# Retention: the decays move from the output to the query, the state's copy, k and the mask

## The chip, the cores and the metric

The kernel runs on one core of one Trainium2 chip. The metric is the device time of one execution in microseconds, the median of three runs.

## The reference

The inputs are q, k and v of shape (8, 8, 576, 64): batch, heads, sequence, head size. Retention is attention with a decay in place of the softmax. It is followed by two feed-forward layers without biases.

```python
scores = scale * np.matmul(q, k.transpose(0, 1, 3, 2))
gamma = 1.0 - 2.0 ** (-5.0 - np.arange(H, dtype=np.float32))
Dmat = np.where(rel >= 0, gamma[:, None, None] ** rel[None, :, :], 0.0)   # rel = i - j
att = np.matmul(scores * Dmat[None], v)          # then to (4608, 512)
h = x @ w_in
x = (h * np.cos(h)) @ w_out                      # 512 -> 2048 -> 512
h = np.maximum(np.maximum(x @ w1, x @ w2), x @ w3)
out = h @ w_out2                                 # 512 -> 768 -> 512
```

## The kernel before

The 4608 tokens are cut into nine blocks of 512. In each block the eight heads are taken as four pairs, so retention consists of 36 units (block j, pair hp), numbered 4j + hp. Inside a unit the tokens are cut into chunks of 128; where a sequence of 576 ends inside a block, two of the chunks are of 64. Blocks 0, 2, 4, 6 and 8 have four chunks, blocks 1, 3, 5 and 7 have three full ones and two short ones.

Because gamma^(i-j) is a product, the kernel never forms the whole decay matrix. Per unit it does this:

- `att_load` (L486) brings q and k by feature and k and v by token into one tile `u`.
- `att_scale` (L492, GpSimd) multiplies v by gamma to the minus position.
- `att_scores` (L504, TensorE) forms the scores of each chunk in PSUM, and `att_mask` (L513, VectorE) multiplies them by a mask of ones and zeros into `ret`.
- `att_state` (L547, TensorE) adds each chunk's product of k and v to a running state in PSUM, and `att_keep` (L531, ScalarE) copies the state out before each chunk for its queries.
- `att_out` (L563 and L575, TensorE) forms the output `po` from `ret` and v and from the kept states and q.
- `att_decay` (L590, VectorE) reads `po` out of PSUM, one instruction for each chunk, and multiplies by gamma to the position of the row; that is the scaled output `k_x`.

The feed-forward products run in one level of Strassen's scheme (seven products of quarters), and each operand is split into a high and a low part. `build_in` takes the differences of quarters (L356, GpSimd in most blocks), rounds them to the high part (L360, ScalarE) and subtracts to get the low part (L364, VectorE). `group_in` runs the products (L385), whose results ScalarE copies (L418, L423, L430, L400) or VectorE adds up (L410). `gate` forms h * cos(h): L448 and L457 on ScalarE, L452 and L460 on VectorE, L453 on GpSimd. Weights are read raw, joined (L176 and L177, VectorE), summed (L183, GpSimd), combined (L190 to L193, VectorE) and split (L200 to L207 on ScalarE, L212 and L216).

The order of the work on each engine is written out by hand. `at(n, fn)` puts a step n slots ahead, and `tick()` issues all steps that are due; each product of `group_in` is one slot. The first 15 slots have no product: units 0 to 4 and the first weights fill them. A unit with start s has its scaling in slot s - 1 (but not before the present one), its scores in s, its mask in s + 1, its states from s + 1 on, its output in s + 5 and its decays in s + 6. Two units start every seven slots. Each engine works through its own list in order.

Of the kernel before, what the change touches and what calls it, by code (L numbers as in the profile page):

```python
# [14 lines left out]
AF = mybir.ActivationFunctionType  # L15
ALU = mybir.AluOpType

B, H, S, D = 8, 8, 576, 64
T = B * S
DM = H * D  # L20
NB = 512
HB = NB // 2
NBLK = T // NB
NPAIR = H // 2
CH = 128
# [14 lines left out]
def chunks_of(j):  # L40

    t0 = j * NB
    cut = (-t0) % S
    segs = [(0, cut), (cut, NB)] if 0 < cut < NB else [(0, NB)]
    out = [(a, min(CH, e - a)) for s, e in segs for a in range(s, e, CH)]
    full = [c for c in out if c[1] == CH]
    short = [c for c in out if c[1] < CH]  # L50
    assert len(short) in (0, 2) and all(n == CH // 2 for _, n in short)
    order = full + short
    col = {a: sum(n for _, n in order[:i]) for i, (a, _) in enumerate(order)}
    return [(a, n, col[a], (t0 + a) % S) for a, n in out]


def column_tokens(j):

    idx = np.zeros(NB, np.int64)
    for a, n, c, _ in chunks_of(j):  # L60
        idx[c : c + n] = j * NB + a + np.arange(n)
    return idx


CG = 0
CM = CG + NPAIR * CH
CM2 = CM + CH
CGS = CM2 + CH
CTV = CGS + NPAIR * 9
NCONST = CTV + NBLK * NPAIR * 8  # L70


def constants():
    gamma = (1.0 - 2.0 ** (-5.0 - np.arange(H, dtype=np.float32))).astype(np.float64)
    c = np.zeros((128, NCONST), np.float64)
    p = np.arange(128)
    for hp in range(NPAIR):
        g = gamma[2 * hp + p // 64]
        c[:, CG + hp * CH : CG + (hp + 1) * CH] = g[:, None] ** np.arange(CH) / math.sqrt(D) / WSCALE
        c[:, CGS + hp * 9 : CGS + (hp + 1) * 9] = g[:, None] ** (64 * np.arange(9))  # L80
    c[:, CM : CM + CH] = np.arange(CH)[None, :] >= p[:, None]
    c[:, CM2 : CM2 + CH] = c[:, CM : CM + CH] * ((np.arange(CH) // 64)[None, :] == (p // 64)[:, None])
    for j in range(NBLK):
        pos = (column_tokens(j) % S).reshape(NB // CH, CH)
        for hp in range(NPAIR):
            for s in range(4):
                for e in range(2):
                    col = CTV + ((j * NPAIR + hp) * 4 + s) * 2 + e
                    c[:, col] = gamma[2 * hp + e] ** (-pos[s].astype(np.float64))
    return c.astype(np.float32)  # L90
# [11 lines left out]
def retention_ffn(ctx: ExitStack, tc: tile.TileContext, att, w_in, w_out, w123, w_out2, cst, out):  # L102
    nc = tc.nc
# [12 lines left out]
    def x4(name, shape, dt=F32):  # L116
        return xpool.tile([128, *shape], dt, tag="x", name=name)

    def bank(name):
        return ps.tile([128, NB], F32, tag="b", name=name)  # L120
# [16 lines left out]
    def at(n, fn):  # L137
        agenda.setdefault(slot[0] + n, []).append(fn)
# [329 lines left out]

    cs = cpool.tile([128, NCONST], F32, name="cs")
    units = {}  # L470
    quarters_of = {}

    def order_of(n):
        return divmod(n, NPAIR)
# [12 lines left out]

    def att_scale(n):

        v = units[n]["kv"][:, 1].rearrange("p (s d) -> p s d", d=64)  # L490
        col = CTV + n * 8
        nc.gpsimd.tensor_tensor(  # L492
            out=v, in0=v, in1=cs[:, col : col + 8].unsqueeze(2).to_broadcast([128, 8, 64]), op=ALU.mult
        )

    def att_scores(n):
        u = units[n]
        qT, kT = u["qk"][:, 0], u["qk"][:, 1]
        u["sc"] = [bank(f"sc{n}_{e}") for e in range(2)]
        for s in range(NB // CH):  # L500
            sl = slice(s * CH, (s + 1) * CH)
            for e in range(2):
                r = slice(64 * e, 64 * e + 64)
                nc.tensor.matmul(u["sc"][e][:, sl], kT[r, sl], qT[r, sl], start=True, stop=True)  # L504

    def att_mask(n):
        u = units[n]
        nfull = sum(m == CH for _, m, _, _ in chunks_of(order_of(n)[0]))
        for e in range(2):
            for at_, k, col in ((0, nfull, CM), (nfull, NB // CH - nfull, CM2)):  # L510
                if k:
                    sl = slice(at_ * CH, (at_ + k) * CH)
                    nc.vector.tensor_tensor(  # L513
                        out=u["ret"][:, e, sl].rearrange("p (s i) -> p s i", i=CH),
                        in0=u["sc"][e][:, sl].rearrange("p (s i) -> p s i", i=CH),
                        in1=cs[:, col : col + CH].unsqueeze(1).to_broadcast([128, k, CH]),
                        op=ALU.mult,
                    )

    def att_keep(n, i):  # L520

        u = units[n]
        j, hp = order_of(n)
        ch = chunks_of(j)
        if i >= len(ch):
            return
        _, m, _, pos = ch[i]
        st = state[:, hp * CH : (hp + 1) * CH]
        if pos:
            um = u["kept"][i] = u["um"][:, len(u["kept"])]  # L530
            nc.scalar.copy(um, st)  # L531
        if pos + m == S:
            nc.scalar.activation(st, cs[:, CM : CM + CH], AF.Copy, scale=0.0)

    def att_state(n, i):

        u = units[n]
        j, hp = order_of(n)
        ch = chunks_of(j)
        if i >= len(ch):  # L540
            return
        kn, v = u["kv"][:, 0], u["kv"][:, 1]
        _, m, c, pos = ch[i]
        if pos + m < S:
            s, p = divmod(c, CH)
            sl = slice(s * CH, (s + 1) * CH)
            nc.tensor.matmul(  # L547
                state[:, hp * CH : (hp + 1) * CH],
                kn[p : p + m, sl],
                v[p : p + m, sl],  # L550
                start=False,
                stop=True,
                skip_group_check=True,
            )

    def att_out(n):
        u = units[n]
        j, hp = order_of(n)
        qT, v = u["qk"][:, 0], u["kv"][:, 1]
        po = u["po"] = bank(f"po{n}")  # L560
        for s in range(NB // CH):
            for e in range(2):
                nc.tensor.matmul(  # L563
                    po[64 * e : 64 * e + 64, s * CH : (s + 1) * CH],
                    v[:, s * CH + 64 * e : s * CH + 64 * e + 64],
                    u["ret"][:, e, s * CH : (s + 1) * CH],
                    start=s == 0,
                    stop=False,
                    skip_group_check=True,
                )  # L570
        for i, um in u["kept"].items():
            _, m, c, _ = chunks_of(j)[i]
            for e in range(2):
                r = slice(64 * e, 64 * e + 64)
                nc.tensor.matmul(  # L575
                    po[r, c : c + m], um[r, r], qT[r, c : c + m], start=False, stop=True, skip_group_check=True
                )

    def att_decay(n):
        u = units.pop(n)  # L580
        j, hp = order_of(n)
        o = quarters_of.setdefault(j, {"name": f"x{j}", "n": NB})
        half = f"k{hp // 2 + 1}"
        if half not in o:
            o[half] = x4(f"{half}_x{j}", [2, NB])
        for _, m, c, pos in chunks_of(j):
            t, cc = divmod(c, HB)
            g = CGS + hp * 9 + pos // 64
            at_ = (hp % 2) * HB + cc
            nc.vector.scalar_tensor_tensor(  # L590
                out=o[half][:, t, at_ : at_ + m],
                in0=u["po"][:, c : c + m],
                scalar=cs[:, g : g + 1],
                in1=cs[:, CG + hp * CH : CG + hp * CH + m],
                op0=ALU.mult,
                op1=ALU.mult,
            )

    def att_unit(n, start):

        at(max(0, start - 1), lambda: att_scale(n))
        at(start, lambda: att_scores(n))
        at(start, lambda: att_keep(n, 0))
        at(start + 1, lambda: att_mask(n))
        for i in range(5):
            at(start + i + 1, lambda i=i: att_state(n, i))
            if i < 4:
                at(start + i + 1, lambda i=i: att_keep(n, i + 1))
        at(start + 5, lambda: att_out(n))
        at(start + 6, lambda: att_decay(n))  # L610

    NUNIT = NBLK * NPAIR

# [74 lines left out]
    for n in range(5):  # L688
        att_unit(n, 2 * n)
# [10 lines left out]
    for k in range(1, NUNIT - 4):  # L700
        if k > 1:
            at(max(0, start_of(k) - 4), lambda k=k: att_load(4 + k))
        att_unit(4 + k, start_of(k))
    for j in range(1, NBLK):
        k = 4 * (j - 1)
# [288 lines left out]
```

## Time and profile before

| what | value |
|---|---|
| median of 3 runs | 1521.58 us (1521.57 to 1521.79) |
| profiled execution, first to last instruction (span) | 1516.2 us |
| median of the runs less the span | 5.4 us |
| TensorE matmul busy | 1454.9 us, 96% |
| VectorE busy | 1224.6 us, 81% |
| ScalarE busy | 726.8 us, 48% |
| GpSimd busy | 268.7 us, 18% |
| mean granted TensorE clock | 0.988 |

The span is counted on the chip's own instructions in one profiled execution; the runs' times also hold what lies before and after them. Busy shares are means over a kernel with several stages: retention with the first half of the first layer comes first, then the rest of that layer, then the second.

### The profile page before, as it was taken

The page shows a single profiled execution, that of the slowest core. Times are in us where ns is not written, and L with a number is a line of the kernel's source. Part 1 is how long each engine was busy: PE and PEld are TensorE (multiplying, and loading weights), DVE is VectorE, ACT ScalarE, POOL GpSimd, SP SyncE. Part 2 cuts the span into 40 slices and gives each one's busy share as a digit, 9 for nine tenths or more (in the row PEclk, how much of TensorE's full clock was granted, in tenths as well). Part 3 has the DMA queues.
Part 4 walks back from the last instruction along what each step waited for, and adds up shares of the span by engine and source line. Part 5 has one row for each costly group of instructions (what it writes and reads, how often), then busy time and mean ns, then how long its engine had stood idle before and what let it go on. Part 6 is the DMA issues. An engine that isn't in the chain of part 4 may idle for free.

```text
span 1516.2 us, 30767 instructions
## 1 busy us (share of the span) xinstructions
PE 1454.9 (96%) x12506; PEld 1416.0 (93%) x12506; DVE 1224.6 (81%) x1759; ACT 726.8 (48%) x1214; POOL 268.7 (18%) x216
## 2 busy tenths in 40 slices
PE   6899999999899997899999999999999999999998
PEld 5798989998889997899999999999999999999998
DVE  6888999989889989999999998656664555538997
ACT  3555555556667755454445444334432333323332
POOL 3344444444222001100000000000000000004221
PEclk9899999999999998999999999999999999999999
DMA  7588888876989984556555568923431110254443
GB/s 292 181 292 304 309 300 301 318 290 240 355 304 364 328 294 156 184 193 215 193 203 195 196 216 323 397 107 119 147 127 48 70 66 34 70 191 163 168 168 138
DMA packets 83084, 324.46 MB, mean 214 GB/s; under 512 B 9216, under 2 KB 9216, under 8 KB 76928
## 3 DMA queue, kind: packets, MB, share of 16 engines
q1 hardware_dynamic: 82944, 322.51, 59.4%
q8 instruction: 98, 1.61, 0.4%
q14 instruction: 42, 0.34, 0.1%
HBM read 190.35 MB, written 132.12 MB: 213 GB/s over the span
## 4 chain that ended last, share of the span: by engine, by line
PE 46%; DVE 6%; issue 3%; DMA 2%; ACT 1%; POOL 0%; DVEq 0%; SPq 0%; ACTq 0%; POOLq 0%
PE wo L795 17%; PE d_b L385 14%; PE b_b L385 7%; PE o L795 4%; PE a_b L385 3%; DVE l_m L768 1%; DMA st_o<-p_o 1%; DVE tb_m L356 1%; DVE o_o L808 1%; DVE x_m L759 1%; DVE u_o L808 1%; DMA raw_b<-w 1%; DVE l_g L768 0%; DMA k_m<-mq 0%; ACT h_m L763 0%
## 5 line engine op out<-in xcount | busy, mean ns | idle before, releaser
L795 PE MATMUL wo<-h_g,w_wo 128*128 128x256 f32 x1728 | 314.9, 284 | 0.0
L795 PEld LDWEIGHTS wo<-h_g,w_wo 128*128 128x128 f32 x1728 | 271.3, 193 | 0.0
L795 PE MATMUL wo<-l_g,w_wo 128*128 128x256 f32 x864 | 246.6, 285 | 7.6 <-DVE l_g L768 7.6
L385 PE MATMUL d_b<-x_z,w_b 128*128 128x256 f32 x1944 | 248.8, 283 | 2.9 <-ACT s_b L430 2.1
L385 PEld LDWEIGHTS d_b<-x_z,w_b 128*128 128x128 f32 x1944 | 239.9, 192 | 3.7 <-ACT s_b L430 2.7
L795 PEld LDWEIGHTS wo<-l_g,w_wo 128*128 128x128 f32 x864 | 166.7, 193 | 9.6 <-DVE l_g L768 9.5
L385 PE MATMUL b_b<-x_z,w_b 128*128 128x256 f32 x972 | 131.6, 283 | 2.0 <-DVE x_z L364 2.0
L385 PE MATMUL d_a<-x_x,w_wi 128*128 128x256 f32 x864 | 123.2, 293 | 4.1 <-DVE x_x L364 2.9
L385 PEld LDWEIGHTS b_b<-x_z,w_b 128*128 128x128 f32 x972 | 123.2, 192 | 2.2 <-DVE x_z L364 2.2
L385 PE MATMUL d_a<-x_y,w_wi 128*128 128x256 f32 x864 | 115.3, 291 | 9.2 <-ACT s_a L418 5.8
L385 PEld LDWEIGHTS d_a<-x_y,w_wi 128*128 128x128 f32 x864 | 110.9, 199 | 10.4 <-ACT s_a L418 6.5
L385 PEld LDWEIGHTS d_a<-x_x,w_wi 128*128 128x128 f32 x864 | 110.2, 195 | 8.9 <-DVE x_x L364 4.1
L795 PE MATMUL o<-h_m,w_o 128*128 128x256 f32 x648 | 117.5, 283 | 0.0
L763 ACT CAST h_g<-tb_g 128x1024 fp32r<-128x1024 f32 x36 | 37.8, 1051 | 150.5 <-DVE tb_g L356 145.9
L795 PEld LDWEIGHTS o<-h_m,w_o 128*128 128x128 f32 x648 | 101.1, 192 | 0.0
L452 DVE SCALAR_TENSOR_TENSOR t_a<-s_a,t_a 128x1024 f32<-128x1024 f32 x72 | 99.8, 1389 | 1.4 <-ACT t_a L448 1.4
L410 DVE TENSOR_TENSOR s_b<-s_b,b_b 128x512 f32<-128x512 f32 (+1 forms) x45 | 28.5, 634 | 87.1 <-PE b_b L385 87.0
L460 DVE TENSOR_TENSOR s_a<-s_a,t_a 128x1024 f32<-128x1024 f32 x72 | 90.6, 1274 | 5.9 <-ACT t_a L457 5.9
L457 ACT ACTIVATE t_a<-t_a 128x1024 f32<-128x1024 f32 x72 | 76.3, 1062 | 34.8 <-DVE t_a L453 25.6
L410 DVE TENSOR_TENSOR s_b<-s_b,a_b 128x512 f32<-128x512 f32 (+1 forms) x45 | 28.5, 634 | 79.2 <-PE a_b L385 69.4
L795 PE MATMUL o<-l_m,w_o 128*128 128x256 f32 x324 | 91.8, 283 | 0.0
L418 ACT COPY s_b<-d_b 128x512 f32<-128x512 f32 (+1 forms) x45 | 24.5, 544 | 127.3 <-PE d_b L385 120.0
(173 smaller groups left out, 3003.1 us busy)
## 6 DMA issues: line engine op xcount, KB each, us to landing
u<-att SPq DMA_DIRECT2D x36, 1024.0 KB, 7.3
gq<-s_a SPq DMA_DIRECT2D x72, 512.0 KB, 6.4
k_g<-gq SPq DMA_DIRECT2D x72, 512.0 KB, 6.6
xs<-x_x SPq DMA_DIRECT2D x63, 512.0 KB, 7.3
x_y<-xs SPq DMA_DIRECT2D x63, 512.0 KB, 7.9
w_b<-st_b SPq DMA_DIRECT2D x8, 1792.0 KB, 13.0
st_b<-p_b SPq DMA_DIRECT2D x27, 512.0 KB, 3.8
raw_b<-w SPq DMA_DIRECT2D x18, 512.0 KB, 6.1
```

The source lines that it names most:

```text
L356: eng.tensor_tensor(out=d, in0=a, in1=b, op=ALU.subtract)
L385: nc.tensor.matmul(h[:, p * HB : (p + 1) * HB], a, b, start=first and p == 0 and i == 0, stop=i == len(terms) - 1, skip_group_check=True,)
L410: nc.vector.tensor_tensor(out=dst, in0=dst, in1=b[:, :n], op=ALU.add)
L418: nc.scalar.copy(s0[:, 0], d[:, :n])
L452: nc.vector.scalar_tensor_tensor(out=r, in0=s, scalar=INV2PI, in1=st["t"], op0=ALU.mult, op1=ALU.subtract)
L457: nc.scalar.activation(r, r, AF.Sin, scale=TURN, bias=HALF_PI)
L460: nc.vector.tensor_tensor(out=s, in0=s, in1=f32(st["t"]), op=ALU.mult)
L759: nc.vector.tensor_tensor(out=o["x"][:, 1], in0=o["k1"][:, 0], in1=f32(o["x"][:, 0]), op=ALU.subtract)
L763: nc.scalar.copy(h, o[pairs[k][2]])
L768: nc.vector.tensor_tensor(out=lo, in0=o[pairs[k][2]], in1=f32(h), op=ALU.subtract)
L795: nc.tensor.matmul(b[:, mt * HB : (mt + 1) * HB], a, v, start=first and mt == 0 and p == 0 and i == 0, stop=last and p == len(ws) - 1 and ...
L808: nc.vector.scalar_tensor_tensor(out=d, in0=b, scalar=scale, in1=other, op0=ALU.mult, op1=ALU.add)
```

## The change

The factor gamma^(i-j) is taken apart in another way. The query is multiplied by gamma to the position inside its chunk (and by the scale) before the scores are formed: `att_queries`, a new step on VectorE in slot s - 1, one instruction in blocks of four chunks, two in the others. The mask is multiplied by a scalar for each row, gamma to the minus position inside the chunk, in the same instruction. GpSimd scales k by token instead of v. The kept copy of the state is multiplied by gamma to the chunk's first position by ScalarE. The output then needs no factor, and ScalarE copies it out of PSUM with one instruction a unit, `att_evacuate`, in the slot that `att_decay` had. The table of constants gets 16 more columns.

```diff
     def att_scale(n):
-        v = units[n]["kv"][:, 1].rearrange("p (s d) -> p s d", d=64)
+        kn = units[n]["kv"][:, 0].rearrange("p (s d) -> p s d", d=64)
         col = CTV + n * 8
         nc.gpsimd.tensor_tensor(
-            out=v, in0=v, in1=cs[:, col : col + 8].unsqueeze(2).to_broadcast([128, 8, 64]), op=ALU.mult
+            out=kn, in0=kn, in1=cs[:, col : col + 8].unsqueeze(2).to_broadcast([128, 8, 64]), op=ALU.mult
         )
+
+    def att_queries(n):
+        qT = units[n]["qk"][:, 0]
+        j, hp = order_of(n)
+        nfull = sum(m == CH for _, m, _, _ in chunks_of(j))
+        for at_, k, w in ((0, nfull, CH), (nfull * CH, 2 * (NB // CH - nfull), CH // 2)):
+            if k:
+                q = qT[:, at_ : at_ + k * w].rearrange("p (s i) -> p s i", i=w)
+                col = CG + hp * CH
+                nc.vector.tensor_tensor(
+                    out=q, in0=q, in1=cs[:, col : col + w].unsqueeze(1).to_broadcast([128, k, w]), op=ALU.mult
+                )
...
     def att_mask(n):
...
-                    nc.vector.tensor_tensor(
+                    g = row + 2 * hp + e
+                    nc.vector.scalar_tensor_tensor(
                         out=u["ret"][:, e, sl].rearrange("p (s i) -> p s i", i=CH),
                         in0=u["sc"][e][:, sl].rearrange("p (s i) -> p s i", i=CH),
+                        scalar=cs[:, g : g + 1],
                         in1=cs[:, col : col + CH].unsqueeze(1).to_broadcast([128, k, CH]),
-                        op=ALU.mult,
+                        op0=ALU.mult,
+                        op1=ALU.mult,
                     )
...
-            nc.scalar.copy(um, st)
+            g = CGS + hp * 9 + pos // 64
+            nc.scalar.activation(um, st, AF.Copy, scale=cs[:, g : g + 1])
...
-    def att_decay(n):
+    def att_evacuate(n):
...
-        for _, m, c, pos in chunks_of(j):
-            t, cc = divmod(c, HB)
-            g = CGS + hp * 9 + pos // 64
-            at_ = (hp % 2) * HB + cc
-            nc.vector.scalar_tensor_tensor(
-                out=o[half][:, t, at_ : at_ + m],
-                in0=u["po"][:, c : c + m],
-                scalar=cs[:, g : g + 1],
-                in1=cs[:, CG + hp * CH : CG + hp * CH + m],
-                op0=ALU.mult,
-                op1=ALU.mult,
-            )
+        at_ = (hp % 2) * HB
+        nc.scalar.copy(o[half][:, :, at_ : at_ + HB], u["po"].rearrange("p (t c) -> p t c", c=HB))
 
     def att_unit(n, start):
         at(max(0, start - 1), lambda: att_scale(n))
+        at(max(0, start - 1), lambda: att_queries(n))
         at(start, lambda: att_scores(n))
...
-        at(start + 6, lambda: att_decay(n))
+        at(start + 6, lambda: att_evacuate(n))
```

## Rows read from the trace of the kernel before

**Rows 1.** Windows: each engine's busy us (and instructions), granted clock, DMA share, GB/s.

```profile
43.00:70.00 27.00, 20.86 (x169) 18.41 (x165) 26.79 (x49) 14.17 (x33) 12.38 (x10) 0.81 0.46 165
70.00:345.00 275.00, 270.42 (x2767) 247.74 (x2764) 245.14 (x398) 162.86 (x331) 120.00 (x101) 1.00 0.85 299
```

**Rows 2.** Four lines' instructions: ns shortest/median/longest, first and last start us, forms.

```profile
L590 DVE SCALAR_TENSOR_TENSOR k_x<-po,cs x160: 269/341/352, 28.0 to 351.9; 128x128 f32<-128x128 f32 x128, 128x64 f32<-128x64 f32 x32
L364 DVE TENSOR_TENSOR x_x<-k_x,x_x x27: 676/682/1786, 37.5 to 361.0; 128x512 fp32r<-128x512 f32 x27
L513 DVE TENSOR_TENSOR u<-sc,cs x104: 274/545/691, 12.0 to 340.3; 128x512 f32<-128x512 f32 x40, 128x384 f32<-128x384 f32 x32, 128x128 f32<-128x128 f32 x32
L418 ACT COPY s_a<-d_a x36: 561/585/591, 45.1 to 564.7; 128x512 f32<-128x512 f32 x36
```

**Rows 3.** Timeline of VectorE, 0 to 70 us: start us, us, line, instructions.

```profile
7.27 0.41 DVE L176 TENSOR_SCALAR t_wi<-t_wi 128x512 uint32<-128x512 uint32 x1
...
8.78 0.69 DVE L177 SCALAR_TENSOR_TENSOR raw_wi<-raw_wi,t_wi 128x512 uint32<-128x512 uint32 x1
...
18.14 0.63 DVE L176 TENSOR_SCALAR t_wi<-t_wi 128x512 uint32<-128x512 uint32 x1
...
28.03 1.12 DVE L590 SCALAR_TENSOR_TENSOR k_x<-po,cs 128x128 f32<-128x128 f32 x4
...
32.17 1.28 DVE L513 TENSOR_TENSOR u<-sc,cs 128x512 f32<-128x512 f32 x2
...
44.85 1.24 DVE L590 SCALAR_TENSOR_TENSOR k_x<-po,cs 128x64 f32<-128x64 f32 x5
...
49.78 0.42 DVE L193 TENSOR_TENSOR s_wi<-fa_wi,s_wi 128x256 f32<-128x256 f32 x1
```

**Rows 4.** Timeline of all engines, 59 to 61 us.

```profile
59.00 1.20 DVE L364 TENSOR_TENSOR x_x<-k_x,x_x 128x512 fp32r<-128x512 f32 x1
...
59.61 1.49 POOL L492 TENSOR_TENSOR u<-u,cs 128x512 f32<-128x512 f32 x1
...
60.13 1.53 DVE L364 TENSOR_TENSOR x_x<-ta_x,x_x 128x512 fp32r<-128x512 f32 x1
```

**Rows 5.** Timeline around the scores of units 12, 17 and 32.

```profile
115.40 1.12 DVE L590 SCALAR_TENSOR_TENSOR k_x<-po,cs 128x128 f32<-128x128 f32 x4
...
115.55 1.16 PE L504 MATMUL sc<-u 64*128 64x128 f32 x16
...
164.31 1.24 DVE L590 SCALAR_TENSOR_TENSOR k_x<-po,cs 128x128 f32<-128x128 f32 x5
...
165.48 1.16 PE L504 MATMUL sc<-u 64*128 64x128 f32 x16
...
305.18 1.24 DVE L590 SCALAR_TENSOR_TENSOR k_x<-po,cs 128x128 f32<-128x128 f32 x5
...
305.35 1.04 POOL L453 TENSOR_SCALAR t_a<-t_a 128x1024 f32<-128x1024 f32 x1 [2.02 <-DVE t_a L452]
...
305.82 1.16 PE L504 MATMUL sc<-u 64*128 64x128 f32 x16
```

**Rows 6.** Timeline of TensorE before 70 us; in brackets idle time before, and releaser.

```profile
9.87 2.08 PE L504 MATMUL sc<-u 64*128 64x128 f32 x16 [3.18 <-DMA u<-att]
...
13.75 2.08 PE L504 MATMUL sc<-u 64*128 64x128 f32 x16
...
33.21 1.16 PE L504 MATMUL sc<-u 64*128 64x128 f32 x16
...
43.38 1.70 PE L385 MATMUL d_a<-x_x,w_wi 128*128 128x256 f32 x12
...
45.01 1.16 PE L504 MATMUL sc<-u 64*128 64x128 f32 x16
...
65.10 0.48 PE L547 MATMUL state<-u 64*128 64x128 f32 x2 [1.96 <-ACT u L531]
```

**Rows 7.** Timeline of TensorE at the end of retention.

```profile
359.17 4.15 PE L385 MATMUL d_a<-x_x,w_wi 128*128 128x256 f32 x20 [1.96 <-DVE x_x L364]
```

More of the change, by code (lines that the diff above doesn't have):

```diff
@@ L69 @@
 CTV = CGS + NPAIR * 9
-NCONST = CTV + NBLK * NPAIR * 8
+CKV = CTV + NBLK * NPAIR * 8
+NCONST = CKV + 2 * H
 def constants():
@@ L82, in constants @@
     c[:, CM2 : CM2 + CH] = c[:, CM : CM + CH] * ((np.arange(CH) // 64)[None, :] == (p // 64)[:, None])
+    for h in range(H):
+        c[:, CKV + h] = gamma[h] ** -p.astype(np.float64)
+        c[:, CKV + H + h] = gamma[h] ** -(p % 64).astype(np.float64)
     for j in range(NBLK):
@@ L507, in att_mask @@
         u = units[n]
-        nfull = sum(m == CH for _, m, _, _ in chunks_of(order_of(n)[0]))
+        j, hp = order_of(n)
+        nfull = sum(m == CH for _, m, _, _ in chunks_of(j))
         for e in range(2):
-            for at_, k, col in ((0, nfull, CM), (nfull, NB // CH - nfull, CM2)):
+            for at_, k, col, row in ((0, nfull, CM, CKV), (nfull, NB // CH - nfull, CM2, CKV + H)):
                 if k:
                     sl = slice(at_ * CH, (at_ + k) * CH)
-                    nc.vector.tensor_tensor(
+                    g = row + 2 * hp + e
+                    nc.vector.scalar_tensor_tensor(
                         out=u["ret"][:, e, sl].rearrange("p (s i) -> p s i", i=CH),
                         in0=u["sc"][e][:, sl].rearrange("p (s i) -> p s i", i=CH),
+                        scalar=cs[:, g : g + 1],
                         in1=cs[:, col : col + CH].unsqueeze(1).to_broadcast([128, k, CH]),
-                        op=ALU.mult,
+                        op0=ALU.mult,
+                        op1=ALU.mult,
                     )
```

## The prediction

> **What bounds the kernel now.** I read the windows first, then the groups of the touched lines, then the timeline of the two stretches in which those lines run. From 70 to 345 us TensorE is busy 270.42 of 275 us and VectorE 245.14: TensorE is the bound, with 4.6 us of idle time in all, and VectorE runs a queue just behind it [rows 1]. The stretch from 43 to 70 us is different: TensorE is busy 20.86 of 27 us at a granted clock of 0.81 (so for part of it at 1.2 GHz, the lower of its two levels), VectorE 26.79, so VectorE's queue decides there [rows 1]. Before 43 us neither is full; units 0 to 4 go through TensorE, ScalarE and back, one matmul of the state at a time. Retention ends with the last decay at 351.9 us [rows 2]; later stages can only shift. The reader should therefore ask two things: what leaves or enters VectorE's queue before 70 us, and what TensorE newly waits for after it.
>
> **Removed.** 160 decays of line 590 leave VectorE. Four in a row take 1.12 us, five 1.24 [rows 3]; 20 units with four and 16 with five make 42.2 us. They read PSUM and one tile of SBUF; none is longer than 352 ns [rows 2].
>
> **Added on VectorE.** The scaled query is an in-place product of 128x512 from two SBUF tiles, the form of line 364: 0.68 us at its median, 1.79 at its longest [rows 2]. Blocks 1, 3, 5 and 7 need two instructions (384 and 128 columns), which I take as 0.70 us. 36 units make 24.8 us, so VectorE is relieved by 17 us if nothing holds the new products. The mask gets a second product by a column of scalars; line 590 is that form and reads PSUM at the same pace, so I take nothing (bounds: 0 and 104 instructions by 0.02 us, on a queue that isn't the bound).
>
> **What holds a two-tile product.** The longest times of line 364 come when GpSimd is in an instruction. At 59.00 us it takes 1.20 us, GpSimd's scaling starts at 59.61, and the next line 364, at 60.13, takes 1.53 and ends only 0.56 us after GpSimd does [rows 4]. So GpSimd also gets in between two products that follow each other. Decays and masks, which read PSUM, never show it [rows 2]. The Trainium skill, "SBUF — State Buffer", section "SBUF: two separate sides", says the same as a rule: a VectorE instruction with two SBUF inputs and a GpSimd instruction share one pair of ports, and whoever starts first has it for the whole instruction. The trace agrees (352 against 1786 ns). By that rule the change swaps work that cannot be held for work that can: a rule against it. Without it my steady term below would be 0.9 us, with it 4.0.
>
> **Moved to ScalarE.** 36 copies of 128x512 out of PSUM, 0.58 us each by line 418 [rows 2], 21 us. From 70 to 345 us ScalarE is busy 162.86 of 275 us [rows 1]; the copy can start when the output's matmuls end, one product (some 1.7 us) before VectorE reached the decay. I take nothing. If that cover fails, the state copies behind it come up to 0.58 us later, with a slot of 1.7 us before TensorE wants them. The state copies keep their form and only get a scale; k's scaling takes over v's place and shape on GpSimd: nothing. The constants grow by 16 columns in 1,092: nothing.
>
> **The new wait.** Scores of a unit now wait for its query, and the query stands in VectorE's queue one slot ahead. Behind it on VectorE stand the evictions of the products and the low halves; behind the scores on TensorE stands every product. In the steady part the query of unit n stands where the decays of unit n-2 stood (both belong to the slot before the scores of n), so the distance from those decays' start to the scores' start is the slack, against 0.68 to 0.70 us of work and, as an estimate, 0.1 to pass it on: 0.80.
> - 14 odd units from 9 on: 0.94 to 1.17 us, as at 164.31 and 165.48 [rows 5]. Enough, with little over.
> - Seven units 10, 14, ..., 34: 1.27 us or more. Enough.
> - Six units 12, 16, ..., 32 (pair 0 of blocks 3 to 8): 0.15, 0.54, 0.25, 0.21, 0.01 and 0.64 us; the first is 115.40 to 115.55, the last 305.18 to 305.82 [rows 5]. Not enough: 6 x 0.80 - 1.80 = 3.0 us of stall. An earlier query in the same busy stretch replaced 1.12 of decays by 0.70, so all are 0.42 earlier: about 0.9 us is left.
> - In these six GpSimd's clamp (line 453, 1.04 us) starts 0.17 us after the decays do [rows 5]. A single query is ahead of it; in blocks 3, 5 and 7 the clamp can get between the two halves, 1.04 us more each: 0.9 + 3.1 = 4.0.
> Bounds 0.9 and 4.0. The row at 60.13 speaks for the upper; I take two of three, **+3.0**. TensorE has no spare time there to give it back.
>
> **The lead-in.** Units 0 to 6, each step from its row:
> - Query 0 heads VectorE's queue and waits for unit 0's load, which starts the scores at 9.87 [rows 6]. Four instructions that join the first weights, 7.27 to 9.47 [rows 3], now follow it: 9.87 + 0.68 + 2.2 = 12.75. Mask 0 (1.28) and query 1 follow: 14.7 unheld, 16 with two holds. Scores 1 go from 13.75 [rows 6] to between 14.75 and 16.
> - Mask 1 and query 2 then let the second join, at 18.14 [rows 3], start 1.4 to 3 us later; I take 2.0.
> - From there VectorE is full. Query 3 enters (0.7), decays 0 leave (1.12): mask 3, 32.17 to 33.44 [rows 3], ends at 35.0, and query 4 at 35.75. Scores 4 stood at 33.21 [rows 6], ahead of that mask: they are now 2.6 us late, and with them the chain of state matmuls and copies to the first product at 43.38 [rows 6].
> - Decays 4 (1.24 at 44.85) leave: +1.4 at the sums that end at 50.2 [rows 3]. Query 5 follows them, so scores 5 go from 45.01 [rows 6] to about 52.3. The products behind them find gaps that were there before. Queries 5 and 6 add 1.4: the state matmul at 65.10 [rows 6], which waits for VectorE's sums through ScalarE, comes **+2.8** us later.
> Bounds: 0, if TensorE's gaps take up everything, and +4.5 with the holds.
>
> **The end of retention.** At 359.17 a product waits 1.96 us for a low half on VectorE [rows 7], a few instructions behind the last four decays, which now leave 1.12 us free: **-1.0** (bounds 0 and -1.96).
>
> **Sum.** 2.8 + 3.0 - 1.0 = +4.8 us. The profiled span goes from 1516.2 to about 1521.0; the median of the runs stands 5.4 us above the span, so 1521.58 becomes 1526.4. A difference under 0.2% (3.0 us) can't be told from none.
>
> **Rivals.**
> - *Absorbed* (no change). The lead-in's gaps, 6 us of idle TensorE [rows 1], take up the late scores, GpSimd does not get between the halves: 0.5 + 0.9 - 1.0, about 1522. For it: in that stretch TensorE waited anyway. Against: scores 4 head a chain without gaps.
> - *VectorE's relief wins* (faster). If VectorE's queue alone sets the stretch to 70 us, decays 0 to 4 (5.7) leave and queries 2 to 6 (3.5) enter: -2.2, with -1.96 at 359.17, and perhaps 2 us from a clock that does not fall to 0.81: about 1516 to 1518. It decides if scores 4 and 5 find their queries without TensorE waiting more than 1 us. Against: their place in the queue.
> - *The port takes more* (much slower). If GpSimd holds most queries (1.33 in place of 0.68), the 14 odd units lack 0.4 us each, 5.7 us, and the six 2 more, the lead-in 1.7: about 1535. The rule named above leads there. Against: in the odd units VectorE has just waited for TensorE, and GpSimd is mostly idle at that point.
>
> **Chances.** The forecast (1523.5 to 1530) 0.55, absorbed 0.28, relief 0.10, port 0.07. The range runs from 1519.5, between relief and absorbed, to 1532. Faster 0.10; slower 0.60 (the forecast's upper nine tenths, the port, a little of absorbed); same 0.30.
>
> **What would show it.** Query instructions that are mostly 0.68 us, some over 1.2 beside GpSimd. TensorE's waits naming the query ahead of scores: at unit 4, at unit 5 by several us, and at units 12, 20 and 28. The first product near 46 us, unit 7's scores near 72 in place of 69.3, and everything after 380 us alike but shifted. Wrong if scores 4 do not move, if the stretch 70 to 345 holds no more idle TensorE than 4.6 us, or if a load or a ScalarE copy turns up in TensorE's waits.

## The result and the profile after

The changed kernel takes 1532.67 us at the median (1527.7 to 1533.98, 4 runs) against 1521.57 before: a ratio of 1.007, 95% interval 1.0052 to 1.0088. It is 11.1 us slower. The forecast was slower by 4.8 us, at 1526.4; the direction came true, the size was more than twice the forecast, and the time lies 0.7 us above the upper end of the range.

The profiled execution took 1533.51 us with a span of 1531.7, so 1.8 us lie outside the span. Runs of the kernel before varied from 1517 to 1525 us in the later comparisons, and the profiled one, with its span of 1516.2, was among the faster. The two spans differ by 15.5 us, 4 us more than the cause below accounts for: from the first product of `wo` on `h_g` (of the output weights `w_out`, behind all of retention), to the end, the 14 profiles of this study take between 939.8 us (before) and 944.5, in no order that follows the edits (943.8 after). So that product's start is the better ruler for single profiles: 576.4 us before, 587.9 after, +11.5.

The shifts along the way, from TensorE's timelines of both kernels (start in us):

| what starts | before | after | shift |
|---|---|---|---|
| scores of unit 0 | 9.87 | 11.01 | +1.1 |
| scores of unit 1 | 13.75 | 17.49 | +3.7 |
| scores of unit 4 | 33.21 | 37.54 | +4.3 |
| first product | 43.38 | 51.48 | +8.1 |
| scores of unit 5 | 45.01 | 56.76 | +11.8 |
| scores of unit 6 | 56.09 | 68.52 | +12.4 |
| scores of unit 7 | 69.33 | 77.10 | +7.8 |
| scores of unit 35 | 335.26 | 347.50 | +12.2 |
| `wo` on `h_g` | 576.4 | 587.9 | +11.5 |

Two stretches lose time: the lead-in (+7.8 to unit 7) and the steady part (+4.5 from there to unit 35). In these two profiles 0.7 us come back afterwards. In the lead-in most of the loss is idle time: up to the scores of unit 7 TensorE was busy for 50.05 of 69.33 us before and for 51.36 of 77.10 after, so 6.5 of the 7.8 us are idle and 1.3 are longer matmuls. TensorE's rows of the lead-in after:

```profile
11.01 2.08 PE L520 MATMUL sc<-u 64*128 64x128 f32 x16 [4.35 <-DVE u L508]
...
17.49 2.08 PE L520 MATMUL sc<-u 64*128 64x128 f32 x16 [2.42 <-DVE u L508]
...
37.54 1.88 PE L520 MATMUL sc<-u 64*128 64x128 f32 x16 [0.66 <-PE state L568]
...
51.48 1.69 PE L389 MATMUL d_a<-x_x,w_wi 128*128 128x256 f32 x12
...
56.76 0.94 PE L520 MATMUL sc<-u 64*128 64x128 f32 x12 [3.60 <-issue]
58.00 0.57 PE L520 MATMUL sc<-u 64*128 64x128 f32 x4 [0.29 <-DVE u L508]
...
68.52 2.08 PE L520 MATMUL sc<-u 64*128 64x128 f32 x16 [3.62 <-issue]
...
77.10 1.16 PE L520 MATMUL sc<-u 64*128 64x128 f32 x16
```

These answer to [rows 6]. Scores 0 waited 3.18 us for a load before and now wait 4.35 us for the query; scores 1 wait 2.42. Scores 5 and 6 stand still for 3.60 and 3.62 us. The releaser of those two is given as "issue", for want of a visible event; but the first halves of their queries end at 56.66 and 68.42 us, 0.1 us ahead of the scores. (The rows of the queries, next, span both halves.)

VectorE and GpSimd in the same stretch (a line with x2 holds two instructions):

```profile
10.27 0.69 DVE L508 TENSOR_TENSOR u<-u,cs 128x512 f32<-128x512 f32 x1 [2.94 <-DMA u<-att]
10.31 1.55 POOL L496 TENSOR_TENSOR u<-u,cs 128x512 f32<-128x512 f32 x1 [9.87 <-DMA u<-att]
10.88 1.26 DVE L180 TENSOR_SCALAR t_wi<-t_wi 128x512 uint32<-128x512 uint32 x1
12.18 0.69 DVE L181 SCALAR_TENSOR_TENSOR raw_wi<-raw_wi,t_wi 128x512 uint32<-128x512 uint32 x1
...
12.74 1.04 POOL L496 TENSOR_TENSOR u<-u,cs 128x512 f32<-128x512 f32 x1 [0.88 <-DMA u<-att]
12.79 1.28 DVE L180 TENSOR_SCALAR t_wi<-t_wi 128x512 uint32<-128x512 uint32 x1
13.74 1.22 POOL L187 TENSOR_TENSOR fa_wi<-raw_wi 128x512 uint32<-128x512 uint32 x1
14.10 1.41 DVE L181 SCALAR_TENSOR_TENSOR raw_wi<-raw_wi,t_wi 128x512 uint32<-128x512 uint32 x1
15.43 1.40 DVE L531 SCALAR_TENSOR_TENSOR u<-sc,cs 128x512 f32<-128x512 f32 x2
16.75 0.68 DVE L508 TENSOR_TENSOR u<-u,cs 128x512 f32<-128x512 f32 x1
...
56.11 1.83 DVE L508 TENSOR_TENSOR u<-u,cs 128x384 f32<-128x384 f32 x2
56.31 1.49 POOL L220 TENSOR_TENSOR w_wi<-s_wi,w_wi 128x512 fp32r<-128x512 f32 x1 [2.12 <-issue]
...
66.51 1.49 POOL L496 TENSOR_TENSOR u<-u,cs 128x512 f32<-128x512 f32 x1
...
67.03 1.59 DVE L508 TENSOR_TENSOR u<-u,cs 128x384 f32<-128x384 f32 x2
```

The four joins of the first weights took 0.41 and 0.69 us at a time before GpSimd had anything to do [rows 3]. Behind query 0 they meet GpSimd's scaling and sums, and three of the four take 1.26, 1.28 and 1.41 us. Query 1 therefore starts at 16.75 and scores 1 at 17.49. Queries 5 and 6 are themselves held: 1.83 and 1.59 us for two instructions that take 0.75 when nothing holds them (unit 7).

The windows (the first of a stretch of the lead-in, the second answering to [rows 1]):

```profile
37.00:52.00 15.00, 12.77 (x120) 10.47 (x121) 8.59 (x16) 7.26 (x17) 1.81 (x2) 0.77 0.33 118
...
80.00:355.00 275.00, 267.43 (x2727) 244.00 (x2726) 230.72 (x304) 181.96 (x353) 124.49 (x100) 1.00 0.85 297
```

In the steady part VectorE is relieved (230.72 of 275 us, where it had 245.14), but TensorE was the bound and lost 3 us (267.43 against 270.42). The touched lines, answering to [rows 2] (shortest, median and longest ns):

```profile
L508 DVE TENSOR_TENSOR u<-u,cs x52: 277/678/1391, 10.3 to 346.1; 128x512 f32<-128x512 f32 x20, 128x384 f32<-128x384 f32 x16, 128x128 f32<-128x128 f32 x16
...
L531 DVE SCALAR_TENSOR_TENSOR u<-sc,cs x104: 331/605/751, 15.4 to 351.8; 128x512 f32<-128x512 f32 x40, 128x384 f32<-128x384 f32 x32, 128x128 f32<-128x128 f32 x32
...
L552 ACT ACTIVATE u<-state,cs x128: 346/368/386, 13.9 to 357.6; 128x128 f32<-128x128 f32 x128
```

The state's copy in the kernel before, for comparison:

```profile
L531 ACT COPY u<-state x128: 237/266/288, 12.7 to 344.7; 128x128 f32<-128x128 f32 x128
```

The query's median is the 0.68 us that was forecast, and the longest is twice that. The mask became 60 ns longer (545 to 605). The state's copy, forecast to keep its form, took 266 ns at the median before and takes 368 now, 128 times. TensorE's waits by releaser (total us, times, longest): after from 0 to 80 us, after from 77 to 348 us, and before between its scores of units 7 and 35 (69.3 to 335.3 us):

```profile
PE sc L520 <- issue: 7.2, 2, 3.6
PE sc L520 <- DVE u L508: 7.1, 3, 4.4
PE state L568 <- ACT u L552: 6.2, 10, 1.6
...
```

```profile
PE state L568 <- ACT u L552: 4.5, 6, 1.1
PE sc L520 <- PE d_a L389: 1.2, 3, 0.4
PE d_a L389 <- DVE x_x L368: 0.7, 3, 0.3
PE sc L520 <- PE a_a L389: 0.5, 2, 0.3
PE sc L520 <- PE state L568: 0.2, 1, 0.2
```

```profile
PE state L547 <- ACT u L531: 3.5, 5, 0.7
PE d_a L385 <- DVE x_x L364: 0.9, 2, 0.5
```

The first two lines hold 14.3 us of waits ahead of scores in the lead-in; unit 0's wait for its load, 3.2 us, was there before. In the steady part TensorE is idle for 7.6 us between the scores of units 7 and 35, where it had been for 4.6: waits ahead of scores (the releasers named are the products just ahead of them) went from 0 to 2.3, and waits of the state matmuls for ScalarE's copies from 3.5 to 4.5.

Two places of the steady part, unit 12 and unit 33, show who holds a query:

```profile
123.79 1.59 DVE L508 TENSOR_TENSOR u<-u,cs 128x384 f32<-128x384 f32 x2
123.95 1.28 POOL L457 TENSOR_SCALAR t_a<-t_a 128x1024 f32<-128x1024 f32 x1 [2.01 <-DVE t_a L456]
...
124.44 1.49 PE L520 MATMUL sc<-u 64*128 64x128 f32 x16
...
326.64 1.30 POOL L360 TENSOR_TENSOR tb_x<-k_x,ta_x 128x512 f32<-128x512 f32 x1
...
327.13 1.36 DVE L508 TENSOR_TENSOR u<-u,cs 128x512 f32<-128x512 f32 x1
...
328.59 0.83 PE L520 MATMUL sc<-u 64*128 64x128 f32 x10 [0.45 <-PE d_a L389]
```

In unit 12 the clamp gets between the two halves of the query, as was feared: the halves need 0.55 and 0.28 us when nothing holds them, and here end 1.59 us after the start. It does so in all six even units of blocks 3, 5 and 7. In unit 33 GpSimd's difference of quarters starts 0.49 us ahead of the query, which then takes 1.36 us and ends only 0.55 us after GpSimd. Differences of the same line stretch the queries (in blocks of two instructions, one of the halves) of units 9, 13, 21, 25, 29, 33 and 35 to between 1.0 and 1.4 us.

### The profile page after: what moved, and what is told of

Read it like the earlier page. It is cut to its first block, busy times and chain, and to the rows that moved or that the text cites. A ratio compares the mean times of both kernels' runs of the same rounds, so it can differ in the third digit from the quotient of the medians.

```text
span 1531.7 us, 30647 instructions
## 1 busy us (share of the span) xinstructions
PE 1457.6 (95%) x12506; PEld 1417.2 (93%) x12506; DVE 1213.9 (79%) x1651; ACT 754.4 (49%) x1250; POOL 276.0 (18%) x216
## 4 chain that ended last, share of the span: by engine, by line
PE 49%; DVE 3%; issue 3%; DMA 2%; ACT 1%; SPq 0%; POOL 0%; DVEq 0%; POOLq 0%; ACTq 0%
PE wo L807 15%; PE d_b L389 14%; PE o L807 9%; PE b_b L389 7%; PE a_b L389 4%; DMA raw_b<-w 1%; DVE l_g L780 1%; DMA st_o<-p_o 1%; DMA k_g<-gq 0%; DMA k_m<-mq 0%; DVE p_b L220 0%; DVE tb_g L360 0%; DVE o_wo L820 0%; DVE ta_g L360 0%; DVE u_wo L820 0%
## 5 line engine op out<-in xcount | busy, mean ns | idle before, releaser
L807 PE MATMUL wo<-l_g,w_wo 128*128 128x256 f32 x864 | 247.3, 286 | 10.2 <-DVE l_g L780 10.2
L807 PEld LDWEIGHTS wo<-l_g,w_wo 128*128 128x128 f32 x864 | 167.2, 194 | 12.4 <-DVE l_g L780 12.3
L389 PEld LDWEIGHTS d_a<-x_y,w_wi 128*128 128x128 f32 x864 | 109.0, 196 | 10.8 <-ACT s_a L422 6.5
L456 DVE SCALAR_TENSOR_TENSOR t_a<-s_a,t_a 128x1024 f32<-128x1024 f32 x72 | 93.0, 1294 | 1.4 <-ACT t_a L452 1.4
L552 ACT ACTIVATE u<-state,cs 128x128 f32<-128x128 f32 x128 | 45.7, 369 | 84.4 <-PE state L568 84.3
```

The source lines that it names most:

```text
L389: nc.tensor.matmul(h[:, p * HB : (p + 1) * HB], a, b, start=first and p == 0 and i == 0, stop=i == len(terms) - 1, skip_group_check=True,)
L456: nc.vector.scalar_tensor_tensor(out=r, in0=s, scalar=INV2PI, in1=st["t"], op0=ALU.mult, op1=ALU.subtract)
L552: nc.scalar.activation(um, st, AF.Copy, scale=cs[:, g : g + 1])
L807: nc.tensor.matmul(b[:, mt * HB : (mt + 1) * HB], a, v, start=first and mt == 0 and p == 0 and i == 0, stop=last and p == len(ws) - 1 and ...
```

## The experiments

The theory was that TensorE's wait for scaled queries costs nearly all of the time, in the lead-in for the larger part. The rivals: that longer copies and masks cost it, that the whole copy on ScalarE does, and that it is GpSimd's holds on VectorE (the prediction's *The port takes more*). Each kernel was run 4 to 10 times beside runs of the kernel before, whose medians there were 1520.80 (e1 to e4), 1521.17 (e5 to e9) and 1521.89 us (the rest), so kernels are compared by the ratio; the last three columns of this table are single profiles (steady: from the scores of unit 7 to those of unit 35). The intervals of e2, e3, e5, e6, e8, e12 and e13 overlap with that of after: where one of these is set against after below, the reading rests on the traces. The steady part repeats well: 270.01 to 270.47 us in the three kernels whose units 7 to 35 are those of after (after, e1, e12), and 265.93 and 266.03 in the two with those of before (before, e2).

| run | median us | ratio to before [95%] | scores of unit 7 | steady, us | `wo` on `h_g` |
|---|---|---|---|---|---|
| before | 1521.57 | | 69.33 | 265.93 | 576.4 |
| after | 1532.67 | 1.0070 [1.0052, 1.0088] | +7.8 | 270.40 | +11.5 |
| e1_first_old | 1526.34 | 1.0035 [1.0022, 1.0048] | -0.3 | 270.01 | +3.3 |
| e2_rest_old | 1529.85 | 1.0056 [1.0038, 1.0074] | +5.2 | 266.03 | +3.9 |
| e3_query_early | 1530.16 | 1.0061 [1.0040, 1.0082] | +7.3 | 268.61 | +8.9 |
| e4_no_query | 1519.93 | 0.9997 [0.9986, 1.0009] | -1.1 | 265.54 | -3.0 |
| e9_query_late | 1523.42 | 1.0015 [1.0005, 1.0026] | +3.4 | 267.77 | +4.8 |
| e5_plain_keep | 1528.96 | 1.0045 [1.0026, 1.0064] | +6.5 | 268.79 | +7.5 |
| e6_plain_mask | 1532.79 | 1.0075 [1.0058, 1.0093] | +6.2 | 269.58 | +10.7 |
| e8_query_pool | 1529.11 | 1.0043 [1.0026, 1.0060] | +6.0 | 268.23 | +7.7 |
| e12_lead_place | 1528.16 | 1.0042 [1.0024, 1.0059] | +2.0 | 270.47 | +6.3 |
| e13_copy_later | 1531.03 | 1.0065 [1.0041, 1.0088] | +6.8 | 268.85 | +9.1 |
| e14_both | 1525.51 | 1.0028 [1.0015, 1.0040] | +3.9 | 267.54 | +4.5 |
| e10_late_plain | 1520.95 | 1.0000 [0.9988, 1.0012] | -0.7 | 265.81 | 0.0 |

### Where: the lead-in or the rest

`e1_first_old` runs units 0 to 6 the old way and the rest the new way; `e2_rest_old` does the reverse with `n >= 7`. The scaling, the mask and the state's copy branch in the same way as the lines shown.

```diff
+    def old(n):
+        return n < 7
...
     def att_queries(n):
+        if old(n):
+            return
...
-        at(start + 6, lambda: att_evacuate(n))
+        at(start + 6, lambda: att_decay(n) if old(n) else att_evacuate(n))
```

> Units 0 to 6 go the way of the kernel before (v scaled, plain mask and state copy, decays on VectorE), units 7 to 35 the new way. Theory A (the queries of the first units stand in VectorE's queue ahead of the scores, and TensorE waits; this is most of the loss): the scores of unit 7 come at 69 to 70 us as before, and the time is before +3 to +5, 1525 to 1527. Rival B (the instructions with a column of scalars, state copy and mask, are longer in every unit, and that is the loss): 29 of 36 units still pay, before +8 to +10, 1530 to 1532. Rival C (the whole copy on ScalarE delays the state copies): the same as B.

> The other half: units 0 to 6 go the new way, units 7 to 35 that of the kernel before. A: the scores of unit 7 come near 77 us, the time is before +6 to +8, 1528 to 1530. B and C: 7 of 36 units pay, before +1 to +3, 1523 to 1525.

Both parts lose time, and each stays where it belongs: with the lead-in old, unit 7 is on time and the steady part takes 270.01 us; with the rest old, unit 7 is 5.2 us late and the steady part takes 266.03, as before. The two ratios add up to 1.0091 where the full change has 1.0070. What the lead-in costs isn't one number: with the same code for units 0 to 6 the first product stood anywhere from 49.1 to 51.5 us (e2, e3, e13 and after). The spread goes with TensorE's granted clock from 37 to 52 us: 0.77 in after, 0.83 in e3, 0.89 in e2 and 0.90 in e13, with the first product at 51.5, 49.5, 49.1 and 49.1 us. In e5, below, the same stretch was granted 1.00, and the first product stood at 47.4:

```profile
37.00:52.00 15.00, 10.67 (x128) 8.60 (x128) 10.44 (x15) 8.11 (x18) 4.00 (x3) 1.00 0.50 181
```

### The place of the queries

`e3_query_early` puts the queries of units 7 and up one slot earlier; `e4_no_query` leaves the scaling of the queries out altogether; `e9_query_late` keeps the same 52 instructions but behind the scores, so that nothing waits for them.

```diff
-        at(max(0, start - 1), lambda: att_queries(n))
+        at(max(0, start - (2 if n >= 7 else 1)), lambda: att_queries(n))
```

> Only the place of the queries of units 7 to 35 is changed: one slot earlier (two slots ahead of the scores). If the steady part's loss is TensorE waiting for queries (2.3 us of idle time ahead of scores there), that idle time goes and the time falls by 2 to 3 us, to 1529 to 1531. If it is the longer instructions, it stays at 1532 to 1533. If the earlier query now waits for its load (two microseconds of margin in five units), VectorE shows that wait and the time rises.

> The scaling of the query is left out of the computation, all else is as in the changed kernel. A: both the waits and 25 us of VectorE's work go; the scores of unit 7 come near 68 us and the time is 1518 to 1522, at or under before. B or C: the longer state copies and masks and the copies on ScalarE remain, 1527 to 1530.

```diff
-        at(max(0, start - 1), lambda: att_queries(n))
...
+        at(start + 2, lambda: att_queries(n))
         at(start + 5, lambda: att_out(n))
```

> The scaling of the queries stays, the same 52 instructions on VectorE, but two slots after the scores and three ahead of the output, so that the scores see the unscaled query (their part of the result lacks that factor). Theory A1 (the loss is TensorE waiting in front of the scores): as without queries, 1519 to 1522, unit 7's scores near 68 to 70 us. Rival A2 (the loss is the work itself, 25 to 33 us on VectorE with its holds by GpSimd): most of the loss stays, 1526 to 1531.

With no query at all the time is that of before: 0.9997, an interval that holds 1. So the masks by a scalar, the scaled state copies, the scaling of k and the whole copies fit into the kernel as long as there is no query; and 42 us of decays taken off VectorE buy nothing, net of these, that can be told from none. With the queries executed late the loss is 2.3 us (0.15% of 1521): that is the price of their work, of the longer copies and of their holds together. The time lies between the two forecasts for e9, 1.4 us above the upper end of A1's. The waits of TensorE in e9, 0 to 72 us, show what is gone:

```profile
PE state L568 <- ACT u L552: 11.1, 12, 2.3
...
PE sc L520 <- DMA u<-att: 3.4, 1, 3.4
```

No scores wait for VectorE any more; scores 0 wait for their load, as before the change. From after to e9 the ratio falls by 0.55%, 8.4 us, and the intervals lie apart. The edit changes nothing but the queries' place, so that is what their place ahead of the scores costs: the wait of the scores, and what the queries push back in VectorE's queue. In the traces, one slot earlier (e3) clears the steady part's waits ahead of scores (2.3 to 0), but only 1.8 us of the 4.5 come back: the query now stands in front of the low halves, and the products' waits for those rise from 0.7 to 1.9 us (77 to 348 us):

```profile
PE state L568 <- ACT u L552: 4.2, 6, 0.8
PE d_a L389 <- DVE x_x L368: 1.9, 5, 0.5
```

### The forms of the copy and of the mask

`e5_plain_keep` copies the state without its scale, `e6_plain_mask` leaves the scalar out of the mask.

```diff
-            nc.scalar.activation(um, st, AF.Copy, scale=cs[:, g : g + 1])
+            nc.scalar.copy(um, st)
```

> The copies of the state lose the column of scalars (the factor of the chunk's first position is left out), so they take 0.27 us again in place of 0.37; all else as in the changed kernel. If the longer copy is hidden: 1531 to 1533, less at most 1 us of the state matmuls' waits. If it sets the chain of the first units: 1526 to 1529.

```diff
-                    nc.vector.scalar_tensor_tensor(
+                    nc.vector.tensor_tensor(
...
-                        scalar=cs[:, g : g + 1],
...
-                        op0=ALU.mult,
-                        op1=ALU.mult,
+                        op=ALU.mult,
```

> The mask loses its column of scalars (the factor by key position is left out), 0.06 us less in each of 104 instructions; all else as in the changed kernel. If VectorE's load ahead of the queries matters: 1 to 2 us less, 1530 to 1531, since three or four masks stand ahead of the late queries of units 4 to 6. If not: 1532 to 1533.

The plain copy is back at the duration of before:

```profile
L552 ACT COPY u<-state x128: 244/266/299, 14.2 to 354.6; 128x128 f32<-128x128 f32 x128
```

and the kernel is 3.7 us faster than after by the medians, 4.0 by the start of `wo` on `h_g`; 1.6 of it lies in the steady part. The two ratios' intervals overlap, so e5 alone doesn't settle it; e10 against e9, below, points the same way. The plain mask buys nothing: 1532.79 against 1532.67.

### The port and the whole copy

`e8_query_pool` moves the queries to GpSimd (one slot earlier from unit 7 on), so that no query stands in VectorE's queue; `e13_copy_later` moves the whole copy of units 7 and up one slot later, which lets GpSimd's differences start later.

```diff
-                nc.vector.tensor_tensor(
+                nc.gpsimd.tensor_tensor(
                     out=q, in0=q, in1=cs[:, col : col + w].unsqueeze(1).to_broadcast([128, k, w]), op=ALU.mult
...
+        at(max(0, start - (2 if n >= 7 else 1)), lambda: att_queries(n))
         at(max(0, start - 1), lambda: att_scale(n))
-        at(max(0, start - 1), lambda: att_queries(n))
```

> The queries go to GpSimd, ahead of the scaling of k, in units 7 to 35 one slot earlier. VectorE is rid of the products and of the holds by the scaling. If VectorE's queue is what makes the scores late: unit 5's scores near 47 to 50 us in place of 56.8, and 1522 to 1527. If GpSimd's queue is no better (its clamp waits for VectorE in front of the query of every other unit): 1530 or more.

```diff
-        at(start + 6, lambda: att_evacuate(n))
+        at(start + (7 if n >= 7 else 6), lambda: att_evacuate(n))
```

> In units 7 to 35 ScalarE's whole copy is issued one slot later, nothing else. Theory: ScalarE frees GpSimd's differences earlier than the decays did, and these now hold the queries of units 9, 21, 25, 29, 33 and 35 (1.0 to 1.4 us in place of 0.68). Then the later copy ends these holds, TensorE's idle time ahead of scores falls from 2.3 to under 1 us between 77 and 347 us, and the time by 1 to 2 us. Rival: the holds come from the scaling of k, so they stay and the time does not change or rises by what the later copy delays.

On GpSimd a query takes 1.27 us at the median, and the lead-in still loses 6.0 us; neither forecast for e8 fits (unit 5's scores start at 52.38 us). TensorE's waits of e8, 0 to 72 us:

```profile
PE state L568 <- ACT u L552: 10.8, 11, 3.2
PE sc L520 <- POOL u L508: 6.1, 2, 5.1
...
PE b_a L389 <- DVE x_x L368: 3.0, 1, 3.0
```

The 5.1 us are ahead of unit 0, which waited 3.2 for its load before; unit 5 waits 1.0, units 1 and 6 not at all. But the waits for state copies, 6.2 us in after, are now 10.8: a wait that is taken out at the scores can come back further down the chain, so the waits ahead of scores alone do not measure the loss.

In e13 the query of unit 33 has GpSimd off its back:

```profile
325.60 0.68 DVE L508 TENSOR_TENSOR u<-u,cs 128x512 f32<-128x512 f32 x1
...
326.54 1.16 PE L520 MATMUL sc<-u 64*128 64x128 f32 x16
...
327.49 2.13 POOL L360 TENSOR_TENSOR tb_x<-k_x,ta_x 128x512 f32<-128x512 f32 x1 [3.10 <-ACT k_x L608]
```

0.68 in place of 1.36 us, and no wait ahead of the scores; over the steady part the waits ahead of scores fall from 2.3 to 0.04 us. GpSimd's difference now starts when the later copy ends; so in after it is the early whole copy that frees it into the query. The price comes back one step on: the differences are late, the products wait 2.0 us for low halves (0.7 in after), and the steady part gains 1.5 of 4.5 us.

### A better order, and what is left without the waits

`e12_lead_place` gives the queries of units 3 to 6 earlier slots; `e14_both` joins e12, e13 and e3; `e10_late_plain` is e9 with the plain state copy.

```diff
-        at(max(0, start - 1), lambda: att_queries(n))
+        if n != 5:
+            at({3: 4, 4: 6, 6: 0}.get(n, max(0, start - 1)), lambda: att_queries(n))
...
         att_unit(n, 2 * n)
+    at(12, lambda: att_queries(5))
```

> The changed kernel with the queries of units 3 to 6 issued earlier on VectorE: 3 one slot, 4 one slot, 5 three slots (ahead of the join, where VectorE had idle time), 6 two slots. If the two waits of 3.6 us in front of the scores of units 5 and 6 are place alone: they vanish, the scores of unit 7 come 3 to 6 us sooner, 71 to 74 us, and the time is 1526 to 1529. If the queries' work and GpSimd's holds in that stretch decide, the waits move to the state or the products and the time stays at 1530 to 1533.

> The places of the queries of units 3 to 6 and the later copy together, and the queries of units 7 to 35 one slot earlier: the best order that keeps the work as it is. By the sum of the single effects 1523 to 1527; not under before, since without any query the kernel only came to before -0.9.

> Queries two slots after the scores and the state copied without its column of scalars; both factors are missing from the parts of the result that need them. If the loss is the wait of the scores (measured 8 to 9 us) and the longer state copy (the rest): before within 1.5 us, 1519.5 to 1522.5. If a third cost is left, such as the whole copy on ScalarE: 1523 or more.

In e12 scores 5 start at 48.06 and scores 6 at 58.78 without a wait ahead of them, in place of 56.76 and 68.52; what is left of the waits, 0 to 76 us, belongs to units 0 and 1:

```profile
PE sc L520 <- DVE u L508: 7.0, 2, 4.6
```

Unit 7 is 2.0 us late and the steady part unchanged. In after, e2, e3 and e13, which leave the queries of units 0 to 6 in their place, it is 5.2 to 7.8 us late, so the 3.6 us waits of units 5 and 6 had not been absorbed (part of the difference may be the clock, which in e12 was granted 1.00 from 37 to 52 us). e14 has e12's places there and is 3.9 us late: TensorE waits 8.3 us for state copies up to unit 7, where it waited 6.2 in after, so not all comes back. The waits of units 0 and 1 stay in both; no run moves the joins ahead of their queries. e14 is the best order with all of the work kept, 1.0028: still slower than before, but clear of after.

e10 is at 1.0000 [0.9988, 1.0012], and `wo` on `h_g` starts where it did before the change. So the place of the queries is 0.55% of the loss of 0.70%. Whose the other 0.15% is stays open. The plain state copy takes it away (e10), as it takes 0.25% off after (e5); but so does leaving out the queries, with the scaled copies kept (e4), and the intervals of e4, e9 and e10 overlap. The masks' scalar costs nothing that shows (e6), nor do the whole copies where no query is in their way (e10). No run has neither decays nor queries and copies the state plainly, so whether relief of VectorE pays for part of the longer copies isn't known. No version tried that keeps the work beats the kernel before.

## Why the prediction was right, and where it failed

**Right.** The scores wait for a query that stands in VectorE's queue; relief of VectorE bought nothing that shows (e4); no load became a new wait of TensorE (VectorE waited 1.26 us for unit 8's, which the scores, 3.4 us later, did not feel). The 0.1 us to pass a query on, an estimate without a row, measured 0.05 to 0.10. The clamp does get between the halves in blocks 3, 5 and 7. *Absorbed* and *VectorE's relief wins* both fall: scores 4 were 4.3 us late, and 5 and 6 stood still.

**Half right: the end of retention, -1.0 forecast.** The wait of 1.96 us [rows 7] fell by 0.6:

```profile
370.95 2.66 PE L389 MATMUL d_a<-x_x,w_wi 128*128 128x256 f32 x20 [1.37 <-DVE x_x L368]
```

A new wait of 0.47 us for a state copy, at 356.30, takes most of that back.

**Failed: the lead-in, +2.8 forecast, +7.8 measured.** Unit 7's scores were to come near 72 us and came at 77.10. The terms were mis-sized in three places.
- Its first steps. The joins behind query 0 were priced at 2.2 us, their time with GpSimd idle. They take 4.5 beside GpSimd's scaling. Scores 1 come 3.7 us late, where 1.0 to 2.25 was forecast, and scores 4 by 4.3 in place of 2.6. The prediction looked for holds on the queries and not on the instructions that the queries push into GpSimd's time.
- Scores 5, forecast at about 52.3, came at 56.76, and 6 behind them. The step said that the products behind them "find gaps that were there before"; they did not: with those two waits taken out, unit 7 is 2.0 (e12) and 3.9 us (e14) late.
- From scores 4 to the first product it took 13.9 us in place of 10.2. Scores 4 and the output matmuls at 39.35, 48.09 and 50.00 are each 0.7 to 0.9 us longer at a granted clock of 0.77, in all some 3.1 us; 0.6 us are longer waits for state copies, which now stand behind the whole copy on ScalarE or take 0.1 us more. In e5 the clock in this stretch was 1.00, and in another, 52 to 77 us, it was 0.73. TensorE had been busy for 21.00 of the 37 us ahead of it in after, and for 21.74 in e5. The kernel before had its low clock later, 0.80 from 52 to 77 us (1.00 from 37 to 52), so that up to unit 7 the longer matmuls come to 1.3 us and no more. No run here settles why the clock fell at one place or the other. The same lead-in cost 5.2 to 7.8 us in four profiles.

**Failed: the state copies, which were to "keep their form" and were put at nothing.** The scale comes from a column of constants, and that form takes 368 ns in place of 266. TensorE waits for these copies one by one in the lead-in and six times in the steady part, so 0.1 us each was not hidden. The "slot of 1.7 us before TensorE wants them" wasn't in the trace of before either: there 3.5 of the 4.6 us of idle time between the scores of units 7 and 35 were waits for these copies. By e9 and e10 their scale costs 2.3 us, by after and e5 3.7; neither pair of intervals lies apart, and e4, which has the scale, loses nothing, so the size isn't settled. The same holds on VectorE, where no one waits: the mask's shortest form went from 274 to 331 ns, although the decays of the kernel before, at 341 ns for 128x128, had shown the price of a scalar column [rows 2]. Reading PSUM "at the same pace" was wrong, with no consequence (e6). The Trainium skill, "ScalarE: Activation LUTs", section "What ACT_TABLE_LOAD costs", gives some 93 ns for each operand that is a column of scalars; the trace agrees, with 102 ns (the instruction also goes from COPY to ACTIVATE).

**Near in size, wrong in place: the steady part, +3.0 forecast, +4.5 measured.** Six even units were to lack slack and 14 odd units to have "enough, with little over". Counted from the end of the instruction ahead to the end of the scores, against before, losses came in only three even units (0.39, 0.34 and 0.59 us in units 12, 24 and 28; in 12 and 28 the clamp stood between the halves, and 0.33 us of each lies inside the scores' row), and in six odd ones: 9, 21, 25, 29, 33 and 35, by 0.18 to 0.52 us. So it is partly luck that the sum came near. The reason given against *The port takes more*, that GpSimd is mostly idle at that point, was true of the trace of before and no longer of the kernel after: before, its differences waited for the decays; now the earlier copy on ScalarE sets them free just ahead of the query (e13). That rival had the mechanism; of its 5.7 us for 14 odd units, 2.1 came, in six. With the even units that makes 3.5 us at the scores. The rest of the steady loss is the state copies: 1.0 us of added waits in the trace, 1.6 by e5.

**Failed: the offset of 5.4 us between the span and the runs.** 2 us lie outside the span, and the profiled run was some 3 us faster than the median. This does not touch the difference.

**Left open.** What in GpSimd's instruction holds VectorE's was never taken away: every version leaves GpSimd beside VectorE. e13 shows the hold for the odd units' queries, by moving the difference out of their way; for the joins of the lead-in it rests on the rows alone.

## What to carry to other kernels

Price an edit by its place, not by the sum of busy times: 25 us of products ahead of TensorE's operand cost 8 us, while 42 us of decays taken away behind its output gave back nothing that shows. When a step in an engine's queue moves, price also what it pushes back into another engine's time, and what a faster releaser sets free and onto whom. An instruction that gains a column of scalars has a new form: take its duration from a row that has one.

## What the runs showed of the hardware that was not expected

- A ScalarE copy of 128x128 out of PSUM takes 368 ns with a column as scale and 266 without (128 of each).
- A VectorE instruction with one tile as input, the join at 10.88 us, takes 1.26 us beside a GpSimd instruction, in place of 0.41 for the first join of before; it ends 0.28 us after GpSimd does.
- GpSimd's clamp, which starts while the first half is running, gets in between two products of VectorE that follow each other in 6 of 6 cases; the second, 128 columns, then takes some 1.12 us in place of 0.28.
- From 37 to 52 us TensorE was granted 0.77 in one profile and 1.00 in another, after 21.00 and 21.74 us of busy time in the 37 us ahead (after and e5).
